# Result tiles inside the chunk's operand tile, result writes moved to the SyncE queue, and a reordered k.v schedule in a fused attention and expert kernel

## The chip, the cores and the metric

One Trainium2 chip, one core. The metric is device time of the program in microseconds (us): the median of the runs. Engines are named as in the profile: PE (TensorE matmul), PEld (its weight loads), DVE (VectorE), ACT (ScalarE), POOL (GpSimd), SP (SyncE). Every engine runs its instructions in program order; SP's instructions here are nearly all DMA issues.

## The reference

Linear attention over 8 batches, 8 heads, 576 tokens, head size 64, then two layers on the 4608 tokens of 512 features. Weights are 64-bit floats on entry.

```python
kv  = einsum('bhsd,bhse->bhde', k, v)
out = einsum('bhsd,bhde->bhse', q, kv)
x   = out / sqrt(mean(out*out, -1) + 1e-6) * g_norm      # per head
h   = ((x @ w1) * (x @ w2)) @ w3 ;  x = h @ w_out         # 512 -> 1024 -> 512
h   = x @ w_in ;  y = (h * sigmoid(h)) @ moe2_w_out       # 512 -> 2048 -> 512
```

## The kernel before, in words

**Stages.** A prologue multiplies w3 by w_out (tiles `wps`, to `wch`, `wcl`), unpacks the 64-bit weights (load, scale, tail, bits, high, low: `wide_*`) and computes attention of chunk 0. Tokens go in nine chunks of 512. Five chunks (`PLAIN` = 0, 1, 3, 5, 7) pass through the first layer at once; the other four (`LATER`) only get their attention here, which is written to DRAM (`xd`) and read back in the second half, which starts at about 468 us and which the change does not touch. All layer matmuls are done in three passes of high and low parts (`passes`, L150 to L152).

**The first layer's loop** has 5 x 8 steps. A step is: matmuls into `pa` (12), into `pb` (12), a first quarter of the previous step's product into `x2ps` (3), then the other three quarters (9). After the eighth step of a chunk the four `x2ps` banks (tag `acc`, 4 buffers) are copied out by ACT and DVE in turn, L702 and L704, to `x2o` tiles (3 buffers for 4 results) and written to `x2d` by DMAs of the POOL queue (L705).

**Events between the matmuls.** Each step has six slots; slot 6 x step + part is worked off after `pa` (parts 0 and 1), after `pb` (2), after the first quarter (3), and at the end of the step (4 and 5). `TIMES` gives for each kind of work the slots of its chunks or batches, the last entry of a row being that of chunk 8 (rows k and l count batches, and their last entry, for a batch 8, is not used): `a` (q times k.v on PE; ACT takes squares `sq` and copies `ob`, 4 buffers, in the order of `DRAIN` 0, 2, 3, 1), `c` (sums of squares on PE, tile `s`), `d`, `e` (the root on ACT and DVE), `r` (PE spreads the factors over `rb`; DVE multiplies into `ob`), `f0`, `f1` (chunk to the operand tiles `xh`, `xl`, or for LATER the DMA of `ob` to `xd`, L490, POOL queue), `k0`, `k3` (k.v matmuls of a batch's row tiles 0 to 2, and 3 and 4), `l0` to `l4` (loads of a batch's five row tiles of k and v, the last with 64 rows; 3 buffers each), `q0` to `q3` (loads of a chunk's q; 4 buffers). Within a slot the order is f0, f1, a, c, d, e, r, k, l, q. Tile buffers of one tag are taken in turn, so a load waits until the tile that had its buffer has been read.

**PSUM.** `pa` and `pb` share two banks (tag `ab`); `a` and `r` use two banks of `att` and these two as well; `s` and the k.v sum `kvps` each take an `att` bank.

**Weight pieces.** `advance()` works one piece of 64-bit weights on: write out what the last piece gave (`flush`, SP queue), load piece n+3 (`raw`, 3 buffers, 512 KB), scale piece n+1 on ACT, bits and differences on DVE. `PACE` says how many advances follow `pa`, the split, and again the split of each step. The first 14 pieces are w1 and w2 of the steps to come (two a step in the first chunk); later ones form blocks for the second half.

**The prologue** is an order by hand (`ORDER`).

Of the kernel before, what the change touches and what calls it, by code (L numbers as in the profile page):

```python
# [7 lines left out]
F32 = mybir.dt.float32  # L8
# [32 lines left out]
PACE = tuple(int(x) for x in """  # L41
# [5 lines left out]
""" if x.isdigit())  # L47
TIMES = {
# [18 lines left out]
}  # L67
# [27 lines left out]
ORDER = """  # L95
load0 load1 load2 kload0 scale0 tail0 load3 scale1 scale2 bits0 tailv1 highv0 tailv2 bits1 low0 kmm0
high1 kload1 low1 hh1 lh1 bits2 qload0 scale3 tail3 highv2 load4 kload2 low2 kmm1 bits3 scale4
hl1 tail4 qload3 highv3 kload3 lh2 kmm2 low3 qload2 qload1 kload4 bits4 high4 hh2 hl2 low4
hl3 kmm3 kmm4 kout0 load5 scale5 tailv5 lh3 bits5 load6 a0 b0 highv5 load7 low5 scale6
tailv6 bits6 scale7 hh3 load8 tail7 highv6 low6 bits7 a1 lh5 b1 high7 load9 scale8 hh5  # L100
c0 tailv8 hl5 hl7 low7 lh7 scale9 tailv9 load10 bits8 d0 bits9 kload5 hh7 load11 high8
scale10 tailv10 low8 load12 high9 e0 hh8 lh8 low9 eh0 bits10 load13 el0 scale11 tail11 high10
bits11 hl8 hl10 r0 low10 hh10 kload6 scale12 load14 tailv12 gload0 highv11 bits12 high12 low11 x0
lh10 lh11 load15 load16 scale13 low12 tail13 r1 hh11 bits13 x1 hl11 highv13 fh0 scale14 tail14
bits14 kload7 hl13 kmm5 scale15 fh1 kmm6 low13 tailv15 scale16 lh13 kload8 hh13 wh0 wh4 wh1
highv14 bits15 low14 kmm7 kload9 high15 wl0 wl1 low15 wh5 kmm8 kmm9 tail16 wl5 lh14 kout1
bits16 hl15 hl14 wl4 fl1 hh14 lh15 hh15 highv16 low16 fl0
"""


@with_exitstack
def fused(ctx, tc, q, k, v, g, w1, w2, w3t, wo1, wb, out):

# [5 lines left out]
    def pool(name, **how):  # L119
        opened[name] = tc.tile_pool(name=name, **how)  # L120
        return opened[name].__enter__()
# [39 lines left out]
    low = const.tile([P, 1], F32)  # L161
    const.tile([P, 79], F32, name="pad_left")
    spread = const.tile([P, P], F32R)
# [190 lines left out]
    def kv_load(b, js):  # L354
        for j in js:
            n = min(P, S - j * P)
            for nm, src in (("k", k), ("v", v)):
                t = at.tile([P, DM], F32, tag=nm, bufs=3, name=f"{nm}{b}_{j}")
                nc.sync.dma_start(out=t[:n], in_=src[b, j * P:j * P + n, :])
                kv_t[nm, b, j] = t, n  # L360

    kvps = {}

    def kv_mm(b, js):
        if js[0] == 0:
            kvps[b] = bank("att", 2, f"kvps{b}")
        for j in js:
            kt, n = kv_t.pop(("k", b, j))
            vt, _ = kv_t.pop(("v", b, j))

            for p in range(KD):
                for i in range(2):
                    f = slice((2 * p + i) * D, (2 * p + i + 1) * D)
                    nc.tensor.matmul(
                        out=kvps[b][i * D:(i + 1) * D, p * D:(p + 1) * D], lhsT=kt[:n, f], rhs=vt[:n, f],
                        start=(j == 0 and p == 0), stop=(j == 4 and p == KD - 1), skip_group_check=True)

    def kv_out(b):
        nc.scalar.copy(out=kv32[b % 2], in_=kvps.pop(b)[:, :KD * D].rearrange("p (a d) -> p a d", a=KD))
# [106 lines left out]
    def att_f(c, i, part=None, eng=None):  # L486
        ps_ = (2 * i, 2 * i + 1)
        if c in LATER:
            for p in ps_:
                nc.gpsimd.dma_start(out=xd[c][:, p, :], in_=o_t.pop((c, p)))  # L490
            return
        if i == 0 and part != 1:
            xt[c] = (xs.tile([P, KD, N], F32R, tag="xh", name=f"xh{c}"),
                     xs.tile([P, KD, N], F32R, tag="xl", name=f"xl{c}"))
        xh, xl = xt[c]
        for p in ps_:
            if part != 1:
                if eng is nc.vector:
                    eng.tensor_copy(out=xh[:, p, :], in_=o_t[c, p])
                else:  # L500
                    nc.scalar.copy(out=xh[:, p, :], in_=o_t[c, p])
            if part != 0:
                nc.vector.tensor_sub(out=xl[:, p, :], in0=o_t.pop((c, p)), in1=xh[:, p, :].bitcast(F32))
# [14 lines left out]

    more = [xs.tile([P, KD, N], U32, tag=x, name=f"more_{x}").rearrange("p a n -> p (a n)") for x in ("xh", "xl")]

# [116 lines left out]
    of["gload"] = g_load  # L637
    idle = at.tile([P, N], F32, tag="x2o", bufs=3, name="idle")
    nc.vector.memset(idle, 0.0)
# [11 lines left out]
    w12_tiles(w12b, range(2, K1))  # L651
    stg = pool(name="stg", bufs=3, reuse_waits="tile")
    cv = pool(name="cv", bufs=3, reuse_waits="tile")
# [32 lines left out]
    def g2_mm(c, j, ms):  # L686
# [6 lines left out]
        if j == K1 - 1 and ms[-1] == KD - 1:  # L693
            for m in range(KD):
                if c != PLAIN[-1]:
                    o = at.tile([P, N], F32, tag="x2o", bufs=3, name=f"x2o{c}_{m}")
                else:
                    if m == 0:
                        o4 = xs.tile([P, KD, N], F32, tag="xh", name=f"x2o{c}")
                    o = o4[:, m, :]  # L700
                if m % 2:
                    nc.vector.tensor_copy(out=o, in_=x2ps[c][m])  # L702
                else:
                    nc.scalar.copy(out=o, in_=x2ps[c][m])  # L704
                (nc.gpsimd if c != PLAIN[-1] else nc.scalar).dma_start(out=x2d[c][:, m, :], in_=o)  # L705
            del x2ps[c]

    def g1_mm(ps_out, wh, wl, xh, xl):
# [9 lines left out]
        "a": att_all, "c": att_c, "d": att_d, "e": att_norm, "r": att_spread,  # L718
        "k0": lambda c: kv_mm(c, [0, 1, 2]), "k3": lambda c: (kv_mm(c, [3, 4]), kv_out(c)),
    }  # L720
# [498 lines left out]
```

## Time and profile before

| | us |
|---|---|
| median of 3 runs (lowest, highest) | 1397.71 (1390.48, 1399.27) |
| profiled execution | 1394.57 |
| its span | 1392.8 |
| PE busy | 1369.9 |
| DVE, ACT, POOL busy | 870.8, 660.1, 347.4 |
| first `pa` matmul (end of the prologue) | 72.26 |

The sum of a prediction is made against the profiled execution, 1394.57 us, which is 1.8 us more than its span. A busy PE in this profile has its pipeline's overlap counted in, so one matmul is shown with 0.39 us although the next starts 0.23 us after it. The clock column (PEclk) is the share of the full TensorE clock that was granted.

### The profile page before, as it was taken

The page shows a single profiled execution, that of the slowest core. Times are in us where ns is not written, and L with a number is a line of the kernel's source. Part 1 is how long each engine was busy: PE and PEld are TensorE (multiplying, and loading weights), DVE is VectorE, ACT ScalarE, POOL GpSimd, SP SyncE. Part 2 cuts the span into 40 slices and gives each one's busy share as a digit, 9 for nine tenths or more (in the row PEclk, how much of TensorE's full clock was granted, in tenths as well). Part 3 has the DMA queues.
Part 4 walks back from the last instruction along what each step waited for, and adds up shares of the span by engine and source line. Part 5 has one row for each costly group of instructions (what it writes and reads, how often), then busy time and mean ns, then how long its engine had stood idle before and what let it go on. Part 6 is the DMA issues. An engine that isn't in the chain of part 4 may idle for free.

```text
span 1392.8 us, 19229 instructions
## 1 busy us (share of the span) xinstructions
PE 1369.9 (98%) x7012; PEld 1143.4 (82%) x7012; DVE 870.8 (63%) x1227; ACT 660.1 (47%) x1032; POOL 347.4 (25%) x238
## 2 busy tenths in 40 slices
PE   7999999999999999999999999999999999999998
PEld 4777777776777888887888888888888889999998
DVE  5955477475774547766764677455754576567468
ACT  5767455463662425514644354544534353543543
POOL 1000100001002040522522444224522352245222
PEclk9999999999999999999999999999999999999999
DMA  9854689897868497798688667866696668888886
GB/s 365 312 191 137 212 279 328 278 316 258 274 222 290 134 312 251 231 326 267 195 269 290 192 196 227 282 192 191 193 301 197 191 207 301 279 254 268 284 254 200
DMA packets 156109, 346.26 MB, mean 249 GB/s; under 512 B 15088, under 2 KB 73456, under 8 KB 156016
## 3 DMA queue, kind: packets, MB, share of 16 engines
q1 hardware_dynamic: 152880, 335.60, 74.5%
q0 software_dynamic: 2560, 8.39, 1.5%
q8 instruction: 56, 0.92, 0.3%
q10 hardware_dynamic: 576, 1.05, 0.2%
q14 instruction: 37, 0.30, 0.1%
HBM read 270.53 MB, written 74.45 MB: 248 GB/s over the span
## 4 chain that ended last, share of the span: by engine, by line
PE 83%; issue 12%; DMA 3%; DVE 1%; ACT 1%; POOL 0%; SPq 0%; DVEq 0%; POOLq 0%; ACTq 0%
PE ps L924 65%; PE wps L608 3%; PE x2ps L150 2%; PE pb L150 2%; PE pb L152 2%; PE pa L150 1%; PE pb L151 1%; PE pa L151 1%; PE pa L152 1%; PE x2ps L151 1%; PE x2ps L152 1%; DMA x2d<-x2o 1%; DMA v<-v_l 1%; DMA more_xl<-wo_l 1%; PE o L406 1%
## 5 line engine op out<-in xcount | busy, mean ns | idle before, releaser
L924 PE MATMUL ps<-xo,w 128*128 128x512 f32 (+1 forms) x2352 | 501.4, 373 | 1.1 <-ACT u L999 1.1
L924 PEld LDWEIGHTS ps<-xo,w 128*128 128x128 f32 x2352 | 431.9, 188 | 67.2 <-ACT u L999 1.5
L924 PE MATMUL ps<-go,w 128*128 128x512 f32 (+1 forms) x2016 | 425.4, 371 | 0.4 <-issue 0.4
L924 PEld LDWEIGHTS ps<-go,w 128*128 128x128 f32 x2016 | 368.7, 188 | 53.4 <-issue 1.0
L816 DVE TENSOR_TENSOR go<-g,go 128x1024 fp32r<-128x1024 f32 (+1 forms) x120 | 136.9, 1143 | 114.5 <-ACT go L815 113.5
L934 DVE TENSOR_TENSOR c<-ps,c 128x512 f32<-128x512 f32 (+1 forms) x280 | 171.2, 639 | 57.6 <-PE ps L924 56.9
L815 ACT CAST go<-g 128x1024 fp32r<-128x1024 f32 (+1 forms) x120 | 115.1, 980 | 49.5 <-PE ps L924 48.3
L803 POOL TENSOR_TENSOR g_t<-g 128x1024 f32<-128x1024 f32 (+1 forms) x48 | 111.1, 2315 | 75.3 <-DVE g L1006 70.4
L803 POOL TENSOR_TENSOR g<-g,g_t 128x1024 f32<-128x1024 f32 (+1 forms) x24 | 53.2, 2215 | 287.7 <-DVE go L816 287.7
L816 DVE TENSOR_TENSOR go<-g_t,go 128x1024 fp32r<-128x1024 f32 (+1 forms) x48 | 81.5, 1698 | 19.7 <-ACT go L815 19.7
L956 ACT COPY s<-ps 128x512 f32<-128x512 f32 (+1 forms) x40 | 21.7, 544 | 143.9 <-PE ps L924 143.9
L934 DVE TENSOR_TENSOR g<-ps,s 128x512 f32<-128x512 f32 (+1 forms) x48 | 30.2, 643 | 66.8 <-PE ps L924 60.7
L150 PE MATMUL x2ps<-ch,wch 128*128 128x512 f32 x160 | 65.4, 409 | 5.3 <-DVE x2o L702 5.3
L857 DVE TENSOR_TENSOR asb<-pb,asb 128x512 f32<-128x512 f32 x40 | 27.5, 688 | 65.9 <-PE pb L152 65.9
L150 PE MATMUL pa<-xh,w12h 128*128 128x512 f32 x160 | 65.0, 407 | 0.1
L151 PE MATMUL pa<-xl,w12h 128*128 128x512 f32 x160 | 63.9, 399 | 0.0
L152 PE MATMUL pa<-xh,w12l 128*128 128x512 f32 x160 | 63.8, 398 | 0.0
L146 DVE TENSOR_TENSOR cl<-asb,ch 128x512 fp32r<-128x512 f32 x40 | 28.2, 706 | 56.3 <-ACT ch L145 56.3
L150 PE MATMUL pb<-xh,w12h 128*128 128x512 f32 x160 | 63.0, 394 | 0.0
L152 PE MATMUL pb<-xh,w12l 128*128 128x512 f32 x160 | 62.5, 390 | 0.4 <-DVE w12l L268 0.4
L152 PE MATMUL x2ps<-ch,wcl 128*128 128x512 f32 x160 | 62.8, 392 | 0.0
L151 PE MATMUL x2ps<-cl,wch 128*128 128x512 f32 x160 | 62.7, 392 | 0.0
(141 smaller groups left out, 1734.1 us busy)
## 6 DMA issues: line engine op xcount, KB each, us to landing
w<-wbd SPq DMA_DIRECT2D x364, 512.0 KB, 4.3
wbd<-bh SPq DMA_DIRECT2D x60, 256.0 KB, 3.5
raw<-wb_l SPq DMA_DIRECT2D x24, 512.0 KB, 5.3
wbd<-s SPq DMA_DIRECT2D x48, 256.0 KB, 3.2
q<-q_l SPq DMA_DIRECT2D x36, 256.0 KB, 4.9
k<-k_l SPq DMA_DIRECT2D x32, 256.0 KB, 5.7
v<-v_l SPq DMA_DIRECT2D x32, 256.0 KB, 5.9
raw<-w_l SPq DMA_DIRECT2D x14, 512.0 KB, 4.8
```

What stands on the lines that cost most here:

```text
L146: nc.vector.tensor_sub(out=l, in0=x, in1=h.bitcast(F32))
L150: nc.tensor.matmul(out=ps_out, lhsT=ah, rhs=bh, start=first, stop=False)
L151: nc.tensor.matmul(out=ps_out, lhsT=ah, rhs=bl, start=False, stop=False)
L152: nc.tensor.matmul(out=ps_out, lhsT=al, rhs=bh, start=False, stop=last)
L608: nc.tensor.matmul(out=wps[m], lhsT=(l if which == "lh" else h)[:, x:x + P], rhs=rhs, start=left[m] == all_of, stop=left[m] == 1)
L803: nc.gpsimd.tensor_tensor(out=x, in0=x if a == place else self.src[a], in1=x if b == place else self.src[b], op=ALU.subtract)
L815: nc.scalar.copy(out=t[:, 0, :, :self.w], in_=x)
L816: self.cuts[n].tensor_tensor(out=t[:, 1, :, :self.w], in0=x, in1=t[:, 0, :, :self.w].bitcast(F32), op=ALU.subtract)
L857: nc.vector.tensor_mul(out=asb, in0=pb, in1=asb)
L924: mm = lambda a, bb, start, stop: nc.tensor.matmul(out=o, lhsT=a, rhs=bb, start=start, stop=stop, skip_group_check=True)
L934: eng.tensor_tensor(out=out_, in0=a, in1=b, op=ALU.add)
L956: nc.scalar.copy(out=t[nm, d], in_=o)
```

## The change

Four results of a chunk go into one tile `xo` that takes the place of the chunk's own `xh` (two tags `xh0`, `xh1` of one buffer each, in turn). They and the `xd` writes are issued by SP: `x2d` writes are put in the list that the next advance flushes, `xd` writes stand in `f0`, `f1`. k and v have 4 buffers; the 64-row tails of k and v lie side by side in DRAM and come in one DMA; two batches share the tile, on partitions 0 to 63 and 64 to 127. All five row tiles of a batch are multiplied in one run, in the slot of `c`. `raw` has 2 buffers. `TIMES`, `PACE` and `ORDER` are new.

```diff
 PACE = tuple(int(x) for x in """
-000 000 000 000 000 000 000 102
-000 121 100 111 002 231 000 113
-100 012 012 010 101 203 110 110
-112 100 030 110 211 000 221 100
-211 030 011 000 000 000 000 000
+000 000 000 000 000 000 000 101
+210 111 000 111 011 202 210 111
+101 003 004 001 100 312 001 000
+401 011 220 000 400 010 220 100
+202 031 011 000 000 000 000 000
...
 TIMES = {
-    "f0": (24, 43, 70, 106, 124, 186, 178, 213),
-    "f1": (25, 46, 72, 95, 127, 160, 182, 213),
-    "a": (2, 27, 57, 81, 111, 135, 165, 182),
-    "c": (9, 30, 65, 87, 116, 142, 171, 189),
-    "r": (15, 39, 69, 93, 123, 147, 177, 212),
-    "k0": (5, 43, 72, 98, 125, 151, 170),
-    "k3": (25, 52, 79, 107, 134, 158, 188),
-    "l0": (0, 16, 67, 84, 119, 142, 175),
-    "l1": (0, 23, 56, 86, 107, 134, 157),
-    "q2": (15, 35, 56, 97, 123, 151, 176),
-    "q3": (18, 29, 62, 90, 117, 158, 171),
+    "f0": (22, 47, 72, 103, 126, 154, 180, 206),
+    "f1": (25, 51, 74, 103, 135, 154, 182, 209),
+    "a": (8, 26, 57, 81, 111, 135, 164, 183),
+    "c": (17, 28, 67, 85, 117, 149, 166, 191),
+    "r": (21, 45, 69, 99, 123, 153, 177, 201),
+    "k": (17, 28, 67, 85, 117, 149, 166),
+    "l0": (5, 15, 29, 72, 109, 131, 163),
+    "l1": (0, 16, 56, 60, 86, 133, 161),
+    "q2": (19, 39, 62, 95, 111, 151, 175),
+    "q3": (18, 21, 50, 86, 108, 153, 166),
...
 ORDER = """
-load0 load1 load2 kload0 scale0 tail0 load3 scale1 scale2 bits0 tailv1 highv0 tailv2 bits1 low0 kmm0
-high1 kload1 low1 hh1 lh1 bits2 qload0 scale3 tail3 highv2 load4 kload2 low2 kmm1 bits3 scale4
-hl1 tail4 qload3 highv3 kload3 lh2 kmm2 low3 qload2 qload1 kload4 bits4 high4 hh2 hl2 low4
-hl3 kmm3 kmm4 kout0 load5 scale5 tailv5 lh3 bits5 load6 a0 b0 highv5 load7 low5 scale6
+load0 scale0 load1 load2 kload0 tail0 scale1 kmm0 kload1 load3 bits0 scale2 tail1 bits1 tail2 highv0
+high1 low1 kload2 lh1 hh1 bits2 load4 low0 scale3 tailv3 high2 hl1 low2 bits3 kmm1 kmm2
+kload3 scale4 tailv4 lh2 high3 bits4 low3 kmm3 hh2 hl2 kload4 high4 kmm4 qload0 load5 kout0
+qload1 scale5 low4 lh3 tailv5 load6 qload2 a0 bits5 qload3 hh3 b0 highv5 load7 scale6 low5
...
     def kv_load(b, js):
         for j in js:
-            n = min(P, S - j * P)
             for nm, src in (("k", k), ("v", v)):
-                t = at.tile([P, DM], F32, tag=nm, bufs=3, name=f"{nm}{b}_{j}")
-                nc.sync.dma_start(out=t[:n], in_=src[b, j * P:j * P + n, :])
-                kv_t[nm, b, j] = t, n
+                if j < 4:
+                    t = at.tile([P, DM], F32, tag=nm, bufs=4, name=f"{nm}{b}_{j}")
+                    nc.sync.dma_start(out=t, in_=src[b, j * P:(j + 1) * P, :])
+                    kv_t[nm, b, j] = t
+            if j == 4:
+                if b % 2 == 0:
+                    kv_t[b // 2] = at.tile([P, 2 * DM], F32, tag="kv4", name=f"kv{b}_{j}")
+                t = kv_t[b // 2][b % 2 * D:(b % 2 + 1) * D, :]
+                nc.sync.dma_start(out=t, in_=kv4[b])
+                kv_t["k", b, j], kv_t["v", b, j] = t[:, :DM], t[:, DM:]
...
         if c in LATER:
             for p in ps_:
-                nc.gpsimd.dma_start(out=xd[c][:, p, :], in_=o_t.pop((c, p)))
+                nc.sync.dma_start(out=xd[c][:, p, :], in_=o_t.pop((c, p)))
             return
         if i == 0 and part != 1:
-            xt[c] = (xs.tile([P, KD, N], F32R, tag="xh", name=f"xh{c}"),
+            xt[c] = (xs.tile([P, KD, N], F32R, tag=f"xh{PLAIN.index(c) % 2}", bufs=1, name=f"xh{c}"),
...
-    stg = pool(name="stg", bufs=3, reuse_waits="tile")
+    stg = pool(name="stg", bufs=2, reuse_waits="tile")
...
             for m in range(KD):
-                if c != PLAIN[-1]:
-                    o = at.tile([P, N], F32, tag="x2o", bufs=3, name=f"x2o{c}_{m}")
-                else:
-                    if m == 0:
-                        o4 = xs.tile([P, KD, N], F32, tag="xh", name=f"x2o{c}")
-                    o = o4[:, m, :]
+                if m == 0:
+                    xo = xs.tile([P, KD, N], F32, tag=f"xh{PLAIN.index(c) % 2}", bufs=1, name=f"xo{c}")
+                o = xo[:, m, :]
                 if m % 2:
                     nc.vector.tensor_copy(out=o, in_=x2ps[c][m])
                 else:
                     nc.scalar.copy(out=o, in_=x2ps[c][m])
-                (nc.gpsimd if c != PLAIN[-1] else nc.scalar).dma_start(out=x2d[c][:, m, :], in_=o)
+                if c == PLAIN[-1]:
+                    nc.scalar.dma_start(out=x2d[c][:, m, :], in_=o)
+                else:
+                    writes.append(dict(out=x2d[c][:, m, :], in_=o))
...
-        "k0": lambda c: kv_mm(c, [0, 1, 2]), "k3": lambda c: (kv_mm(c, [3, 4]), kv_out(c)),
+        "k": lambda c: (kv_mm(c, range(5)), kv_out(c)),
```

## Rows read from the trace of the kernel before

**Rows 1.** The page's first part: engine busy us (share of the span) xinstructions.
```profile
PE 1369.9 (98%) x7012; PEld 1143.4 (82%) x7012; DVE 870.8 (63%) x1227; ACT 660.1 (47%) x1032; POOL 347.4 (25%) x238
```

**Rows 2.** Windows: stretch, us, busy of each engine, PEclk, DMA share, GB/s.
```profile
9.20:72.20 63.00, 56.65 (x380) 41.84 (x381) 50.69 (x67) 41.31 (x60) 0.00 (x0) 1.00 0.95 353
```

**Rows 3.** Waits of PE: us in total, times, longest us.
```profile
PE kvps L374 <- DMA v<-v_l: 6.8, 5, 2.5
PE x2ps L150 <- DVE x2o L702: 5.3, 2, 3.3
PE wps L608 <- DVE woh L578: 1.9, 1, 1.9
```

**Rows 4.** Timeline of DVE and PE: start us, us, instruction [idle before <-releaser].
```profile
243.81 0.68 DVE L702 COPY x2o<-x2ps 128x512 f32<-128x512 f32 x1
...
249.07 0.69 DVE L702 COPY x2o<-x2ps 128x512 f32<-128x512 f32 x1 [4.58 <-DMA x2d<-x2o]
...
249.82 0.50 PE L150 MATMUL x2ps<-ch,wch 128*128 128x512 f32 x1 [2.00 <-DVE x2o L702]
...
336.75 0.79 PE L150 MATMUL x2ps<-ch,wch 128*128 128x512 f32 x1 [3.30 <-DVE x2o L702]
```

**Rows 5.** Windows behind the two waits for x2o, columns as in Rows 2.
```profile
250.60:257.30 6.70, 6.70 (x43) 5.34 (x43) 5.13 (x10) 2.35 (x5) 1.18 (x3) 0.50 0.85 278
...
336.80:342.60 5.80, 5.80 (x14) 4.54 (x15) 2.40 (x4) 0.62 (x1) 2.67 (x5) 0.50 1.03 361
```

**Rows 6.** Timeline of PE around three runs of k.v matmuls.
```profile
9.29 0.69 PE L374 MATMUL kvps<-v,k 128*64 128x64 f32 x16 [2.50 <-DMA v<-v_l]
9.91 0.96 PE L608 MATMUL wps<-woh,w3h 128*128 128x512 f32 x3
...
80.06 1.62 PE L374 MATMUL kvps<-v,k 128*64 128x64 f32 x48 [0.25 <-ACT ob L418]
81.60 0.50 PE L150 MATMUL pa<-xh,w12h 128*128 128x512 f32 x1
...
157.94 0.39 PE L151 MATMUL x2ps<-cl,wch 128*128 128x512 f32 x1
158.17 0.39 PE L152 MATMUL x2ps<-ch,wcl 128*128 128x512 f32 x1
158.49 1.30 PE L374 MATMUL kvps<-v,k 128*64 128x64 f32 x32
```

**Rows 7.** Timeline of PE, the last k.v tile of the prologue.
```profile
60.62 0.68 PE L374 MATMUL kvps<-v,k 64*64 64x64 f32 x16 [1.61 <-DMA v<-v_l]
```

**Rows 8.** Waits of the SP queue: us in total, times, longest us.
```profile
SPq L359 <- PE kvps L374: 44.1, 6, 16.0
...
SPq L198 <- ACT z L211: 24.7, 9, 4.5
...
SPq L383 <- PE o L406: 10.6, 2, 7.6
```

**Rows 9.** Timeline of PE, SP and ACT around `a` of chunk 3.
```profile
166.08 2.20 PE L406 MATMUL o<-q,kv 64*64 64x192 f32 x32
...
167.20 0.33 SPq L383 DMA_DIRECT2D q<-q_l  x1
...
168.66 0.61 ACT L418 COPY ob<-o 128x512 f32<-128x512 f32 x1
...
170.41 0.40 PE L150 MATMUL pa<-xh,w12h 128*128 128x512 f32 x1
```

**Rows 10.** DMA issues: out<-in queue xcount, KB each, median us to landing.
```profile
raw<-w_l SPq DMA_DIRECT2D x14, 512.0 KB, 4.8
...
x2d<-x2o ACTq DMA_DIRECT2D x4, 256.0 KB, 2.4
```

**Rows 11.** The tile `xd`: issue ns min/median/max, first and last; landing.
```profile
L490 POOL DMA_DIRECT2D xd<-ob x16: 539/539/689, 139.0 to 433.5; - x16
...
DMA to landing us min/median/max: 2.7/6.1/11.5
```

More of the change, by code (lines that the diff above doesn't have):

```diff
@@ L95, with fused @@
 ORDER = """
-load0 load1 load2 kload0 scale0 tail0 load3 scale1 scale2 bits0 tailv1 highv0 tailv2 bits1 low0 kmm0
-high1 kload1 low1 hh1 lh1 bits2 qload0 scale3 tail3 highv2 load4 kload2 low2 kmm1 bits3 scale4
-hl1 tail4 qload3 highv3 kload3 lh2 kmm2 low3 qload2 qload1 kload4 bits4 high4 hh2 hl2 low4
-hl3 kmm3 kmm4 kout0 load5 scale5 tailv5 lh3 bits5 load6 a0 b0 highv5 load7 low5 scale6
[L100 to L107, printed above, removed]
+load0 scale0 load1 load2 kload0 tail0 scale1 kmm0 kload1 load3 bits0 scale2 tail1 bits1 tail2 highv0
+high1 low1 kload2 lh1 hh1 bits2 load4 low0 scale3 tailv3 high2 hl1 low2 bits3 kmm1 kmm2
+kload3 scale4 tailv4 lh2 high3 bits4 low3 kmm3 hh2 hl2 kload4 high4 kmm4 qload0 load5 kout0
+qload1 scale5 low4 lh3 tailv5 load6 qload2 a0 bits5 qload3 hh3 b0 highv5 load7 scale6 low5
+tailv6 bits6 a1 scale7 highv6 load8 tailv7 load9 b1 bits7 hl3 lh5 c0 hh5 scale8 highv7
+low6 hl5 hl7 tail8 low7 scale9 tailv9 bits8 load10 bits9 d0 load11 high8 scale10 tailv10 e0
+low8 load12 high9 scale11 eh0 low9 tailv11 el0 load13 scale12 hh7 lh7 hh8 lh8 load14 bits10
+high10 r0 hl8 bits11 low10 highv11 tail12 bits12 hl10 load15 high12 kload5 lh10 scale13 low11 x0
+hh10 r1 tail13 lh11 load16 fh0 low12 hh11 bits13 x1 hl11 highv13 scale14 tail14 bits14 gload0
+scale15 hl13 kload6 tail15 kmm5 high14 fh1 low13 kmm6 lh13 kload7 hh13 wh1 low14 wh0 kload8
+bits15 kmm7 high15 wl0 wh4 scale16 wl1 kmm8 wh5 tailv16 low15 bits16 kload9 kmm9 lh14 hl14
+lh15 fl0 highv16 low16 hh15 hl15 wl5 hh14 wl4 fl1 kout1
 """
 @with_exitstack
-def fused(ctx, tc, q, k, v, g, w1, w2, w3t, wo1, wb, out):
+def fused(ctx, tc, q, k, v, kv4, g, w1, w2, w3t, wo1, wb, out):
     nc = tc.nc
@@ L161, in fused @@
     low = const.tile([P, 1], F32)
-    const.tile([P, 79], F32, name="pad_left")
+    const.tile([P, 72], F32, name="pad_left")
     spread = const.tile([P, P], F32R)
@@ L367, in kv_mm @@
         for j in js:
-            kt, n = kv_t.pop(("k", b, j))
-            vt, _ = kv_t.pop(("v", b, j))
+            kt, vt = (kv_t.pop((x, b, j)) for x in "kv")
             for p in range(KD):
@@ L374, in kv_mm @@
                     nc.tensor.matmul(
-                        out=kvps[b][i * D:(i + 1) * D, p * D:(p + 1) * D], lhsT=kt[:n, f], rhs=vt[:n, f],
+                        out=kvps[b][i * D:(i + 1) * D, p * D:(p + 1) * D], lhsT=kt[:, f], rhs=vt[:, f],
                         start=(j == 0 and p == 0), stop=(j == 4 and p == KD - 1), skip_group_check=True)
@@ L517, in of_pair @@
         return ts[j // 2][:, (j % 2) * N:(j % 2) * N + n * N]
-    more = [xs.tile([P, KD, N], U32, tag=x, name=f"more_{x}").rearrange("p a n -> p (a n)") for x in ("xh", "xl")]
+    more = [xs.tile([P, KD, N], U32, tag=x, bufs=n, name=f"more_{x}").rearrange("p a n -> p (a n)")
+            for x, n in (("xh1", 1), ("xl", 2))]
     def wide_load(n):
@@ L637, in fused @@
     of["gload"] = g_load
-    idle = at.tile([P, N], F32, tag="x2o", bufs=3, name="idle")
+    idle = at.tile([P, N], F32, tag="ob", bufs=4, name="idle")
     nc.vector.memset(idle, 0.0)
@@ L1194, in blocks, with rows @@
         return bits(np.concatenate([a, b]))
+    def rows(x):
+        return x.transpose(0, 2, 1, 3).reshape(B, S, DM)
     arrays = {
         "q_l": lay(q.transpose(1, 3, 0, 2).reshape(KD, P, NCH, N).transpose(2, 0, 1, 3)),
-        "k_l": lay(k.transpose(0, 2, 1, 3).reshape(B, S, DM)),
-        "v_l": lay(v.transpose(0, 2, 1, 3).reshape(B, S, DM)),
+        "k_l": lay(rows(k)[:, :4 * P]),
+        "v_l": lay(rows(v)[:, :4 * P]),
+        "kv4_l": lay(np.concatenate([rows(x)[:, 4 * P:] for x in (k, v)], axis=2)),
         "g_l": lay(g_norm),
```

14 rows, old and new, of the table TIMES are left out of this document.

## The prediction

> **What bounds the kernel now.** First the page's busy shares: PE works 1369.9 of 1392.8 us [rows 1]. So the kernel is bound by PE's own matmuls, and a change that removes no matmul can win only what PE loses: idle time (22.9 us), time at the lower clock, and time lost between matmuls. Then the waits of PE say whose fault the idle time is [rows 3]: 6.8 us for loads of v (prologue), 5.3 us for a DVE copy of a chunk's result, 1.9 us for an unpacked weight. The timeline of the 5.3 us shows two waits of 2.00 and 3.30 us, and what ended the first: the fourth copy to `x2o` sat 4.58 us idle, until the DMA that wrote the first result out had landed, because four results share three buffers [rows 4]. Last the granted clock: behind each of the two waits stands a stretch at 0.50 of 2.4 GHz, 1.2 GHz, of 6.7 and 5.8 us, in which PE has work all the time [rows 5]. At half clock half of it is lost, 3.4 and 2.9 us. After the waits of 1.9 and 1.61 us in the prologue [rows 3, 7] the window shows a clock of 1.00 [rows 2]. So a wait of two microseconds stands just where the trace shows the clock fall, and costs 3 us more if it does.
>
> **The change part by part.** The sum starts at this execution's 1394.6 us, 3.1 us under the median of 1397.71, which I read as spread (the three runs span 8.8).
>
> *Own tile for results.* All four copies can follow each other: the third ended at 243.81 + 0.68 = 244.49, a fourth of 0.69 ends at 245.18, and PE wanted that bank at 249.82 - 2.00 = 247.82 [rows 4], 2.6 us later. The tile's former content, `xh`, has been read by then, and the next writer of that tag is `f0` two PLAIN chunks on (results of chunk 0 at slots 48 to 53, `f0` of chunk 3 at 72), so no wait replaces the old one. Both waits go with their slow stretches: 2.00 + 3.30 + 3.4 + 2.9 = **-11.6 us**. What could be late next is DVE itself with more advances ahead of it; 2.6 us of cover are left, so I keep a low end of -6 (one of the two survives).
>
> *k.v in the run of the sums.* A run of these full-precision matmuls pays at both ends. Going in: 158.17 to 158.49 is 0.32 us against 0.23 between like matmuls, 0.09 more. Going out: a run of 16 takes 0.62 (9.29 to 9.91), one of 48 takes 1.54 (80.06 to 81.60), so 16 cost 0.46 and 0.16 belongs to the end [rows 6]. The loop has `k0` and `k3` for batches 2 to 7, twelve visits, one of which already stands against `a`; all now fall into the run of `c`: 11 x 0.25 = **-2.7 us** (-1.0 if only the entry is saved). The sums' chain to `r` is covered by the 80 matmuls of k.v.
>
> *Prologue.* The last k.v tile waited 1.61 us for v [rows 7], and the loads of k and v stood 44.1 us behind buffers not yet read, up to 16.0 at once [rows 8]. With four buffers a batch's loads find them free, so this 1.61 goes. Of the other prologue waits (6.8 - 1.61 of the v loads, 1.9 for the weight) 2.5 is the start, which keeps its order of loads. The remaining 2.7 of v and 1.9 compete for the same transfers at a DMA share of 0.95, and DVE is busy 50.69 of 63 us [rows 2]; moving loads forward moves others back. I take 0.9 of the 4.6: **-2.5 us** in all; ends -6.2 (all of it) and +2 (the new order makes PE wait for one more weight, as the 1.9 did).
>
> *Writes on SP.* 32 issues leave POOL, where each took 0.54 us [rows 11]; as SP issues of about 0.4 us they are 13 us of SP time over 310 us, in a queue that idles in waits. That by itself costs nothing. But a write now stands in line behind SP's waits, and at one place this counts. `q3` of chunk 4 is set at slot 50, but its buffer holds q of chunk 3, which is read by `a` at slot 57: SP stands there from 50 to 57. Such a wait exists before: 7.6 us [rows 8], ended by the same `a` (the load at 167.20 [rows 9]). Now `f1` of chunk 2, slot 51, is behind it: the writes of two `ob` tiles. And `a` of chunk 3 needs those very buffers for its second copy on ACT, and `pa` needs the bank which that copy frees. In the times of before: `a` ends at 166.08 + 2.20 = 168.28; q issue and write issue 0.8; landing; copy 0.61; `pa` would have started at 170.41 [rows 9]. For the landing the rows give 2.4 us (the same write on a quiet hardware queue [rows 10]) to 6.1 (median of these writes, which go out among others [rows 11]). SP has been standing, so I stay near the lower one and add 0.6 for the q load just ahead of it (256 KB at the 353 GB/s of the prologue is 0.7): 3.0. Then 168.28 + 0.8 + 3.0 + 0.61 = 172.7, about 0.4 of which the hand-overs overlap: **+1.9 us**, ends 1.3 and 5. The clock may fall or not; I forecast that it does not, and keep 3.4 us for the range.
>
> The Trainium skill (DMA: Bandwidth & Descriptors, section "Queues, rings and completion order") says that a DMA engine takes the descriptors of one ring in order and serves the rings in turn, so a write from POOL's ring would not sit behind SP's q load. By that rule these 0.6 us are the price of the move and the stall left on POOL's ring would be 1.3, the sum 1379.1; no row here separates the two.
>
> *Two raw buffers.* Load n+3 now waits for scale n+1 instead of n: one advance later. In the first chunk two advances fill a step of about 7.8 us, and the piece is scaled two advances after its issue: 7.8 us against a landing of 4.8 [rows 10]. Cover 3 us, cost nothing; beyond it ACT waits and weights come late: up to +2. SP already spends 24.7 us on this wait [rows 8]. Later pieces load in pairs with four advances between, where two buffers never meet.
>
> *One tail DMA a batch* is 8 issues less on SP, hidden like them; the 64-row matmuls stay. Nothing.
>
> Sum: 1394.6 - 11.6 - 2.7 - 2.5 + 1.9 = **1379.7 us**.
>
> **The rivals.**
> *Clock falls at the new wait* of `a`: 1379.7 + 3.4 = 1383.1. For it: it fell after 2.00 us. Against: it held after 1.9. Chance 0.25.
> *One more wait like it*: the new `PACE` has four advances in a row at slot 144 and a chunk end just behind, so either the old x2o wait survives once by DVE's queue, or an ACT wait for `raw` reaches PE. One wait of 2.0 with its 3.4: 1383.1 + 5.4 = 1388.5. Chance 0.17.
> *SP becomes the bound; slower.* All results, block writes and loads now pass one in-order queue, in which `l1` of batch 5 (slot 60) waits for the k.v of batch 4 (slot 67) and the like. If the raw load or a result write behind such a wait arrives after ACT's cover, PE stalls and the clock falls: 5.4 us each. With the prologue's loss of 2 instead of its gain (+4.5), and four such places: 1379.7 + 4.5 + 21.6 = 1405.8. It passes the profiled time from three places on. Against: in the trace SP stood 44.1 us for buffers [rows 8] and PE paid for it only in the prologue. Chance 0.07.
> *The change doesn't do what it says at `a`*: if the buffers free earlier than I read it, no wait, and the prologue wins all: 1394.6 - 11.6 - 2.7 - 6.2 = 1374.1. Chance 0.11.
>
> **How the numbers follow.** The forecast has 0.40, the rivals 0.25, 0.17, 0.07 and 0.11. A measurement of this kernel can tell about 1% from no change: 1383.7 is the line for faster, 1411.7 for slower. Faster: 0.40 (less 0.04 for its upper side), 0.11, and half of the 0.25 that sits on the line: 0.59. Slower: the upper part of the SP case, 0.04. Same: 0.37. The range from 1373 to 1392 leaves out the SP case and the tails of the outer two.
>
> **What would show it.** The idle time before L702 for its own write gone, and no stretch at 0.50 behind the ends of chunks 1 and 3; no separate k.v runs; first `pa` at about 69.8 instead of 72.3; a PE wait of about 1.9 us before `pa` of the step after `a` of chunk 3, ended by ACT's `ob`, itself ended by the DMA `xd`. If the `x2ps` wait remains, the step on the tile is wrong; if SP-issued writes land late in several places, the step on SP is.

## The result: 1374.3 us beside 1394.1, and the profile after

The changed kernel takes 1374.30 us (median of 4 runs, 1373.15 to 1376.72), the kernel before 1394.10 beside it: ratio 0.9859, 95% interval 0.9836 to 0.9881. The forecast was 1379.7, range 1373 to 1392. The profiled execution is the slowest of the four, 1376.72 with a span of 1374.9.

Busy time, first part of the page after, beside [rows 1]:

```profile
PE 1364.1 (99%) x7012; PEld 1142.5 (83%) x7012; DVE 873.9 (64%) x1225; ACT 661.2 (48%) x1034; POOL 331.5 (24%) x206
```

PE has the same 7012 matmuls and is idle for 10.8 us instead of 22.9. Its waits after, beside [rows 3]:

```profile
PE kvps L378 <- DMA v<-v_l: 3.7, 3, 2.2
PE idle_ps L647 <- DVE idle L644: 1.5, 1, 1.5
PE ps L929 <- ACT u L1004: 0.6, 1, 0.6
PE wps L613 <- DVE w3l L596: 0.5, 1, 0.5
```

No wait for `x2ps` is left. The windows (stretch, us, busy of PE, PEld, DVE, ACT, POOL, PEclk, DMA share, GB/s) show the first-layer loop (first `pa` to last `x2ps`) after and before, and the prologue after:

```profile
16.20:26.40 10.20, 9.46 (x52) 5.85 (x52) 4.62 (x7) 1.27 (x3) 0.00 (x0) 0.50 1.04 396
9.20:72.20 63.00, 59.60 (x365) 42.90 (x361) 49.09 (x65) 39.28 (x57) 0.00 (x0) 0.92 0.93 335
73.10:451.00 377.90, 377.58 (x2258) 295.66 (x2257) 235.96 (x433) 203.36 (x371) 10.77 (x4) 1.00 0.77 256
```
```profile
72.30:468.00 395.70, 388.05 (x2256) 298.96 (x2255) 232.71 (x431) 201.91 (x368) 26.95 (x36) 0.98 0.72 242
```

The loop went from 395.8 to 377.6 us: -18.2, all of the gain. PE now idles 0.3 us in it, at a clock of 1.00. The prologue of this execution lost 0.9 (first `pa` at 73.1, before 72.3), for with a wait of 2.24 us for v comes a stretch of 10.2 us at 0.50, which [rows 2] do not have. The rest is 0.5 shorter. Together -17.85 against the profiled 1394.57.

Where the 18.2 went is worked out from the starts of all PE matmuls of the loop, start to start, each compared with the usual step of its kind and place in a run: the two waits for `x2o` with their slow stretches [rows 4, 5] about -11.8, the edges of the k.v runs -3.4, `rb` -2.6, other short waits -0.4.

The chunk end that waited 2.00 us [rows 4] has its two DVE copies back to back now, and a batch's k.v stands in the run of the sums `s` (`kvps<-kv` is the tail tile of k and v). Timeline after of PE and DVE (start us, us, instruction), beside [rows 4, 6]:

```profile
121.09 1.06 PE L429 MATMUL s<-sq,ones 128*32 128x512 f32 x8
122.08 2.08 PE L378 MATMUL kvps<-v,k 128*64 128x64 f32 x64
124.10 0.68 PE L378 MATMUL kvps<-kv 64*64 64x64 f32 x16
124.71 0.50 PE L149 MATMUL pa<-xh,w12h 128*128 128x512 f32 x1
125.05 0.39 PE L150 MATMUL pa<-xl,w12h 128*128 128x512 f32 x1
125.28 0.39 PE L151 MATMUL pa<-xh,w12l 128*128 128x512 f32 x1
...
241.21 1.28 DVE L704 COPY xo<-x2ps 128x512 f32<-128x512 f32 x2
```

Around `a` of chunk 3, timeline after of SP, ACT and PE, beside [rows 9]:

```profile
165.72 0.35 SPq L387 DMA_DIRECT2D q<-q_l  x1
166.10 0.91 SPq L494 DMA_DIRECT2D xd<-ob  x2
...
166.22 0.58 ACT L422 COPY ob<-o 128x512 f32<-128x512 f32 x1
...
167.17 0.60 ACT L422 COPY ob<-o 128x512 f32<-128x512 f32 x1
...
168.69 0.40 PE L149 MATMUL pa<-xh,w12h 128*128 128x512 f32 x1
...
169.29 0.59 ACT L422 COPY ob<-o 128x512 f32<-128x512 f32 x1 [1.01 <-DMA xd<-ob]
```

SP stood 7.64 us until the q load (from the end of the issue before, at 158.07), as forecast; but the third copy waits for the write, not the second, and `pa` starts with no wait. SP's queue after, waits (us in total, times, longest), beside [rows 8]:

```profile
SPq L387 <- PE o L410: 16.9, 4, 7.1
SPq L358 <- PE kvps L378: 10.6, 2, 5.4
...
SPq L387 <- DMA v<-v_l: 3.3, 3, 1.4
...
SPq L358 <- DMA k<-k_l: 1.8, 3, 1.0
```

The standing for k.v fell from 44.1 to 10.6 us. e8b, with four k and v buffers under the old tables, has 0.3, so the buffers (or the single tail DMA beside them) took it, and the earlier load slots brought some back. The two rows that wait for another load are no buffer waits; the last section says what they are.

### The profile page after: what moved, and what is told of

Its sections match the earlier page's. It is cut to its first block, busy times and chain, and to the rows that moved or that the text cites. A ratio compares the mean times of both kernels' runs of the same rounds, so it can differ in the third digit from the quotient of the medians.

```text
span 1374.9 us, 19175 instructions
## 1 busy us (share of the span) xinstructions
PE 1364.1 (99%) x7012; PEld 1142.5 (83%) x7012; DVE 873.9 (64%) x1225; ACT 661.2 (48%) x1034; POOL 331.5 (24%) x206
## 4 chain that ended last, share of the span: by engine, by line
PE 96%; DMA 2%; DVE 0%; ACT 0%; SPq 0%; issue 0%; ACTq 0%; DVEq 0%
PE ps L929 66%; PE x2ps L149 3%; PE wps L613 3%; PE pb L151 3%; PE x2ps L150 3%; PE pa L149 3%; PE pb L149 3%; PE x2ps L151 3%; PE pb L150 3%; PE pa L150 3%; PE pa L151 3%; PE kvps L378 1%; PE o L410 1%; DMA wraw<-w3t_l 1%; PE s L429 1%; DMA kv<-kv_l 1%
## 5 line engine op out<-in xcount | busy, mean ns | idle before, releaser
L808 POOL TENSOR_TENSOR x_t<-x2r 128x1024 f32<-128x1024 f32 (+1 forms) x14 | 32.5, 2323 | 422.3 <-DMA w<-wbd 421.8
L144 ACT CAST ch<-asb 128x512 fp32r<-128x512 f32 x40 | 25.3, 633 | 78.4 <-DVE asb L862 78.4
```

Source lines behind the costliest of these rows:

```text
L144: nc.scalar.copy(out=h, in_=x)
L808: nc.gpsimd.tensor_tensor(out=x, in0=x if a == place else self.src[a], in1=x if b == place else self.src[b], op=ALU.subtract)
```

## The experiments

All times are medians; ratios are against the kernel before on the same chip, with 95% intervals. That kernel took 1394.0 us beside e1 to e4, 1391.4 beside e5 to e8b and 1393.6 beside e9 to e12, so differences between medians of different chips are good to 2 or 3 us only. "Loop" and "first `pa`" are from each one's profiled execution. The intervals of the kernels near 1374 overlap; differences of about 2 us between them are not resolved. Each loop is a single execution.

| | us | ratio | loop | first `pa` |
|---|---|---|---|---|
| before | 1394.1 | 1 | 395.8 | 72.3 |
| changed | 1374.30 | 0.9859 [0.9836, 0.9881] | 377.6 | 73.1 |
| e1 tile alone | 1388.89 | 0.9961 [0.9941, 0.9980] | 388.6 | 72.6 |
| e2 queue alone | 1392.18 | 0.9989 [0.9971, 1.0006] | 392.5 | 71.9 |
| e8b old tables | 1388.53 | 0.9973 [0.9954, 0.9993] | 385.7 | 74.7 |
| e11 three slots | 1386.09 | 0.9946 [0.9930, 0.9962] | 390.1 | 70.3 |
| e3 writes on POOL | 1376.31 | 0.9865 [0.9836, 0.9893] | 380.1 | 69.4 |
| e7 `f0` behind | 1377.30 | 0.9894 [0.9862, 0.9925] | 381.0 | 69.5 |
| e4 split runs | 1383.22 | 0.9917 [0.9885, 0.9948] | 383.7 | 70.3 |
| e12 `r` at 93 | 1373.72 | 0.9858 [0.9843, 0.9874] | 378.7 | 69.5 |
| e9 three raw | 1374.25 | 0.9863 [0.9843, 0.9882] | 377.5 | 71.2 |
| e5 old order | 1375.73 | 0.9875 [0.9844, 0.9906] | 376.8 | 70.5 |
| e6 late k.v | 1373.38 | 0.9863 [0.9833, 0.9894] | 377.6 | 70.0 |
| e10 k.v load first | 1375.39 | 0.9867 [0.9852, 0.9882] | 377.3 | 72.2 |

**e1, the tile alone**, on the kernel before (the tags of `xh` and of two prologue tiles change with it):

```diff
...
-                if c != PLAIN[-1]:
-                    o = at.tile([P, N], F32, tag="x2o", bufs=3, name=f"x2o{c}_{m}")
+                if m == 0:
+                    xo = xs.tile([P, KD, N], F32, tag=f"xh{PLAIN.index(c) % 2}", bufs=1, name=f"xo{c}")
+                o = xo[:, m, :]
...
```

> The kernel before with one part of the change: the four results of a chunk go into the chunk's own xh tile; their writes stay on POOL's queue, all tables are those of before. Theory (the tile removes the waits, the queue is not needed for that): both x2ps<-x2o waits (2.00 and 3.30 us) and the two stretches at 0.50 behind them are gone, 11.6 us less than before, about 1382 to 1384 beside 1394. Rival (the writes on POOL land so late that f0 of a later chunk waits for them, or the wait only moves): a wait of f0's ACT or DVE copy on DMA x2d shows, and less than 5 us is won. Second rival (the change of tables was needed as well): the gain is there, but another PE wait of 2 us or more takes part of it.

It wins 5 us (7.2 in the loop of the profiled execution), not 11.6: the second rival. The first wait and its stretch are gone; in the place of the second PE waits as long for something else. Timeline and window of e1:

```profile
337.78 1.30 PE L374 MATMUL kvps<-v,k 128*64 128x64 f32 x32 [3.28 <-DMA v<-v_l]
```
```profile
339.20:342.50 3.30, 3.30 (x9) 2.52 (x9) 2.42 (x6) 2.58 (x6) 0.00 (x0) 0.50 0.17 55
```

The loads of v for this run are issued at 325.8 and 328.5, and between 324.0 and 328.0 POOL issues the four results and three `xd` writes, now all at once. The tile `v` from 318 to 342 in e1:

```profile
DMA to landing us min/median/max: 9.1/9.2/9.4
```

Before, the fourth copy's wait held back both that burst and PE; the same v loads took 6.1 and 7.7 us, landed by 339.6, and were not needed until 345.9. The x2o wait had been hiding a late load.

**e2, the queue alone**: three x2o buffers, their writes on SP.

```diff
-                (nc.gpsimd if c != PLAIN[-1] else nc.scalar).dma_start(out=x2d[c][:, m, :], in_=o)
+                (nc.sync if c != PLAIN[-1] else nc.scalar).dma_start(out=x2d[c][:, m, :], in_=o)
```

> The kernel before with the queue alone changed: the writes of the results go out on SP's queue, still from three x2o buffers for four results; the xd writes stay on POOL. Theory (the buffers are the cause, the queue only shortens or lengthens the landing): the fourth copy still waits for the first write, PE waits 1 to 4 us at two or more chunk ends and the clock falls behind those over 2 us; the time is 1390 to 1400, within 5 us of before. Rival (POOL's late issue is the cause): the waits of 2.00 and 3.30 go, and the time is about 1383 as with the tile. Second rival: SP stands behind a buffer at a chunk end, and the wait grows beyond 4 us: slower than 1400.

The theory holds in the main: the time is not distinguishable from before, and DVE's fourth copy still waits for a write. But PE pays at one chunk end, where two or more were expected, with 5.05 us where at most 4 were expected; the wait of 2.00 [rows 4] is gone. Timeline of DVE and PE in e2:

```profile
333.31 0.69 DVE L702 COPY x2o<-x2ps 128x512 f32<-128x512 f32 x1 [8.50 <-DMA x2d<-x2o]
...
334.06 0.80 PE L150 MATMUL x2ps<-ch,wch 128*128 128x512 f32 x1 [5.05 <-DVE x2o L702]
```

**e8b, the changed tiles and buffers under the tables of before**: the changed kernel with `PACE`, `TIMES`, `ORDER` and the two runs `k0` and `k3` of the kernel before, and with the writes on POOL:

```diff
...
-nc.sync.dma_start(out=xd[c][:, p, :], in_=o_t.pop((c, p)))
+nc.gpsimd.dma_start(out=xd[c][:, p, :], in_=o_t.pop((c, p)))
-writes.append(dict(out=x2d[c][:, m, :], in_=o))
+nc.gpsimd.dma_start(out=x2d[c][:, m, :], in_=o)
...
```

> The changed kernel's tiles and buffers (results in the chunk's tile, four k and v buffers, one tail DMA, two raw buffers) with the tables of the kernel before (PACE, TIMES, ORDER, k.v in two runs), and with the writes on POOL's queue. Theory (the tables were needed too: the v load is issued too late by its slot, whatever the buffers): a PE wait for v of 1 to 3.5 us at the end of chunk 3 remains, and the time is 1385 to 1389, like the tile alone. Rival (four buffers suffice): no wait for v over 1 us in the loop, no stretch at 0.50, 1380 to 1384. Second rival (two raw buffers need the new PACE): ACT waits for raw and a new PE wait for asb or a weight of 1 us or more shows.

The theory holds: the wait for v shrinks and stays, without a slow stretch behind it. Timeline of e8b:

```profile
338.22 0.69 PE L379 MATMUL kvps<-v,k 128*64 128x64 f32 x16 [1.25 <-DMA v<-v_l]
```

So the buffers and the single tail DMA, which e8b does not tell apart, are part of the answer and the earlier load slots the rest: in the changed kernel the same batch's last loads land by 301.7 and are used at 313.6. Of the loop's 18.2, the tiles and buffers give 10.1 (to 385.7). The other 8.1 are the tables, with k.v in one run, and the move to SP together: 5.6 to e3 (380.1), whose writes are still on POOL, and 2.5 from there, which e3 does not resolve. The time gains only 2.9 us beside its own before (1391.4). Of the difference to the loop, 2.4 lie in the prologue of the profiled execution, where two stretches of 3.4 us at 0.50 stand behind waits of 1.57 and 1.94 us; the rest stays open.

**e11, three slots again under the new tables**, on e3:

```diff
-                o = xo[:, m, :]
+                o = xo[:, m if c == PLAIN[-1] else m % 3, :]
```

> The changed kernel with the writes on POOL's queue and the four results of a chunk put into three slots of the tile again: the fourth copy waits until the first write has been read out, as in the kernel before. Theory (the missing fourth buffer costs the waits, under the new tables as under the old): a PE wait before x2ps of 1.5 to 4 us, ended by that copy, at two to four chunk ends, with a stretch at 0.50 behind those over 2 us; 5 to 14 us more than with four slots and the writes on POOL (1376.3), so 1381 to 1390. Rival (the new PACE alone moved the chunk ends away from late landings): at most one wait under 1.5 us, and 1378 or less.

9.8 us more than e3, within the theory's 5 to 14, but paid elsewhere. DVE's waits (us in total, times, longest) and the timeline of DVE and PE in e11:

```profile
DVE xo L704 <- DMA x2d<-xo: 16.1, 4, 5.9
```
```profile
399.23 0.69 DVE L704 COPY xo<-x2ps 128x512 f32<-128x512 f32 x1 [4.00 <-DMA x2d<-xo]
...
401.93 0.75 DVE L457 SCALAR_TENSOR_TENSOR rhl<-u,low,rh 128x512 fp32r<-128x512 f32 x1 [0.69 <-ACT rh L453]
...
402.74 0.59 PE L467 MATMUL rb<-rhl,spread 32*128 32x512 f32 x3 [3.19 <-DVE rhl L457]
```

DVE stands at all four chunk ends (before: 4.57, 4.58, 6.74 and 0.79 us). Here PE wants `rb` before it wants the bank, and `rhl`, the operand of the `rb` matmuls, is made by DVE behind that copy: the same cause under another name, and a list of PE's waits alone would not have led to the tile. About 6.6 of the 10 us that the loop lost stand at this place (the wait and a stretch of 6.8 us at 0.50). About 3 more stand at 275, far from a chunk end, where `rb` waits 1.67 us for `asb` and a stretch of 3.4 us at 0.50 follows; e3 waits 0.57 us there, and why e11 waits longer stays open. (`asb` is the tile into which ACT copies `pa` and DVE multiplies `pb`; until then their banks are taken.)

**e3, the writes back on POOL**, on the changed kernel: the two write lines of e8b's diff.

> The changed kernel with the writes of x2d and xd given back to POOL's queue, all else as changed. Theory (in the sum the move to SP costs nothing for PE, and ACT's 1.0 us wait at `a` of chunk 3 comes from a write behind the blocked q load): that wait is gone or under 0.5 us, PE shows no new wait, and the time is that of the changed kernel within 2 us, about 1374. Rival (the move brought part of the 18 us that the loop won): 3 us or more of the loop come back, 1377 or more. Rival of the prediction's other side (SP's queue delays loads): 2 us or more less, 1372 or below.

ACT's wait at `a` is gone. The median is 2.0 us more (0.8 by the ratios), within the intervals; the loop is 2.5 longer, most of it by two new waits for `asb` (1.11 at 291.8 and 0.57 at 271.5) at places without a write. What the move to SP is worth by itself lies between nothing and about 2.5 us; these runs do not settle it.

**e7, `f0` of chunk 2 behind the q load**, on the changed kernel:

```diff
-    "f0": (22, 47, 72, 103, 126, 154, 180, 206),
+    "f0": (22, 51, 72, 103, 126, 154, 180, 206),
```

> The changed kernel with f0 of chunk 2 moved from slot 47 to 51, so that all four xd writes of the chunk stand behind the q load for which SP waits until `a` of chunk 3. Theory (the prediction's mechanism at `a` is right, and PE was spared only since two of the four buffers were written out ahead of that q load): the first ob copy of `a` of chunk 3 now waits for a landing about 3 us after the q load is released, PE waits 1.5 to 4 us before the next pa, with 0 to 4 us of lower clock behind it, and the time is 1376 to 1381. Rival (the copies of `a` have more slack than that): ACT waits, PE does not, and the time is that of the changed kernel within 1.5 us.

The mechanism of the prediction appears as soon as all four writes stand behind that load. Timeline of SP, ACT and PE in e7, and the window behind the wait:

```profile
162.03 0.34 SPq L387 DMA_DIRECT2D q<-q_l  x1
162.42 2.05 SPq L494 DMA_DIRECT2D xd<-ob  x4
...
165.75 0.59 ACT L422 COPY ob<-o 128x512 f32<-128x512 f32 x1 [3.11 <-DMA xd<-ob]
...
167.43 0.50 PE L149 MATMUL pa<-xh,w12h 128*128 128x512 f32 x1 [2.26 <-ACT ob L422]
```
```profile
168.90:172.20 3.30, 3.30 (x9) 2.58 (x8) 2.29 (x5) 2.76 (x6) 0.00 (x0) 0.50 1.00 342
```

2.26 us of wait and about 1.7 of slow clock (half of 3.4); the loop is 3.4 us longer, the median 3.0.

**e4, k.v split away from the sums**, on the changed kernel:

```diff
-    "k": (17, 28, 67, 85, 117, 149, 166),
+    "k0": (18, 30, 67, 86, 120, 150, 168),
+    "k3": (20, 32, 68, 88, 122, 152, 170),
```

> The changed kernel with a batch's k.v matmuls split again into two runs that stand away from the sums (three row tiles, then two), eleven runs more in the loop. Theory (a run of these matmuls costs 0.09 going in and 0.16 going out): 11 x 0.25 = 2.7 us more in the loop (3 with the slower first matmul behind a run), about 1377. Rival (the ends cost nothing, what the loop won came from the tables): the loop has the same length within 1 us. Second rival (the two visits hold the k and v buffers longer and SP stands longer): a load of raw or q comes late, and PE waits 1 us or more in a place of its own.

The loop is 6.1 us longer, twice the theory. Compared start to start, the edges of the eleven runs give 2.9 us of it, 0.27 each, about what the theory said. Idle time grows by 2.5, most of it in waits such as these, the first rows of a timeline of e4:

```profile
289.51 0.50 PE L150 MATMUL pb<-xh,w12h 128*128 128x512 f32 x1 [0.79 <-DVE asb L863]
...
295.96 0.86 PE L411 MATMUL o<-q,kv 64*64 64x384 f32 x8 [1.06 <-DVE asb L863]
```

The median is 8.9 us above the changed kernel, 2.8 more than the loop of the profiled execution explains (which is the fastest of its four); that part stays open.

**e12, `r` of chunk 4 back in slot 93**:

```diff
-    "r": (21, 45, 69, 99, 123, 153, 177, 201),
+    "r": (21, 45, 69, 93, 123, 153, 177, 201),
```

> The changed kernel with `r` of chunk 4 in slot 93, as before, instead of 99, one table entry. Theory (the waits of rb for asb in the kernel before came from the slots of r against DVE's backlog, and the new slots took them away): at that place the steps of rb grow by 0.4 to 1.5 us together with a wait for DVE's asb, nothing else moves, and the time stays within 1.5 us of the changed kernel, 1373 to 1377. Rival (the new PACE took them away, wherever r stands): rb's steps stay at 1.95 us for all 24.

A wait is back at that place, though for `rhl`, which DVE had not reached, and not for `asb`. Timeline of e12:

```profile
224.16 1.00 PE L467 MATMUL rb<-rhl,spread 32*128 32x512 f32 x4 [1.10 <-DVE rhl L457]
```

The slot counts, by DVE's backlog there; 1.1 us of loop, too little for the median. The other two `rb` waits of before were not tried in this way.

**e9, three raw buffers** (two more unused pads go as well, for room):

```diff
-    stg = pool(name="stg", bufs=2, reuse_waits="tile")
+    stg = pool(name="stg", bufs=3, reuse_waits="tile")
-    const.tile([P, 72], F32, name="pad_left")
...
```

> The changed kernel with three raw buffers again (some unused padding given up for their room). Theory (two buffers cost nothing: ACT's waits for raw are covered before PE): the loop has 377.6 us within 1 and the time is that of the changed kernel within 1.5, 1373 to 1376. Rival (ACT's waits for raw of 1.43 and 1.24 us are paid somewhere by PE): the loop is 1 to 2 us shorter. Second rival (earlier loads collide with those of k, v and q): a PE wait of 1 us or more for one of these shows.

The theory holds: ACT's waits for the later `raw` pieces are 8.0 us in all instead of 9.0, and neither loop nor time moves.

**e5, e6, e10, the prologue's order**: the `ORDER` of before; the last k.v matmuls later; the first k.v load earlier.

```diff
 e6:
-... kmm3 hh2 hl2 kload4 high4 kmm4 qload0 load5 kout0 qload1 scale5 low4 lh3 ...
+... hh2 hl2 kload4 high4 qload0 load5 qload1 scale5 low4 lh3 kmm3 kmm4 kout0 ...
 e10:
-load0 scale0 load1 load2 kload0 tail0 ...
+load0 scale0 kload0 load1 load2 tail0 ...
```

> The changed kernel with the prologue order of the kernel before (ORDER), all else as changed. Theory (the buffers, not the order, took the wait of 1.61 us for v; the order is worth about 1 us): the first pa stands at 70 to 72 us, the loop is as in the changed kernel (377.6 within 1), and the time is 1374 to 1377. Rival (the order alone wins, the buffers nothing): the wait of 1.6 us for v before the last k.v tile is back and the first pa stands at 72 or later. Second rival (the new order costs, its k.v matmuls stand too early for their loads): no wait for v over 1.5 us, no stretch at 0.50 in the prologue, first pa before 69.7, and the time 1373 or less.

> The changed kernel with the k.v matmuls of row tiles 3 and 4 and the copy of the sum moved behind lh3 in the prologue's order, just ahead of its `a`. Theory (the wait of 2.24 us for v before row tile 3 is due to the place of these matmuls alone, and the clock fell behind it): that wait is gone or under 0.7, no stretch at 0.50 in the prologue, first pa at 67.5 to 69.5, time 1370 to 1373. Rival (the transfers bound the prologue, whatever is multiplied first): another wait of the same size stands elsewhere, first pa at 69.7 to 73, time as the changed kernel within 1.5. Second rival (the matmuls were cover for the unpacking of the weights): waits for hh, hl or `a` grow, and it is 2 us or more slower.

> The changed kernel with the first loads of k and v moved ahead of the second and third weight load of the prologue. Theory (transfers bound the start: what comes earlier for k.v comes later for the weights): the first k.v run begins at 6.5 to 7.5 instead of 8.6, the first wps 1 us or more later, first pa at 69 to 71, and the time within 1.5 us of the changed kernel. Rival (PE's late start is the price, 1 to 3 us of waiting before the first k.v run, with the lower clock that stood behind it in the profile of the changed kernel): first pa at 67 to 68.5 and 1370 to 1372.5.

None differs from the changed kernel by more than the intervals allow. In e5 the wait of 1.61 us [rows 7] is gone under the old order, so the buffers or the single tail DMA took it, as the theory said. In e6 and e10 a wait leaves one place and comes back at another: timeline of e6, then waits of PE in e10.

```profile
21.66 1.19 PE L410 MATMUL o<-q,kv 64*64 64x512 f32 x8 [1.39 <-ACT kv L383]
...
25.47 1.08 PE L410 MATMUL o<-q,kv 64*64 64x512 f32 x4 [1.04 <-DMA q<-q_l]
```
```profile
PE wps L613 <- DVE w3l L596: 3.2, 1, 3.2
PE o L410 <- DMA q<-q_l: 2.2, 1, 2.2
```

With transfers busy for 0.92 or more of the stretch from 9.2 to 69.2 us in every one of these orders, an order chooses who waits. In e10 the first k.v matmul starts at 7.50 with no wait, and the first `wps` then waits 3.2 us. No version is distinguishably faster than the changed kernel.

## Why the prediction was right, and where it was not

The time is faster by over 1%, as I held likeliest, and within the range; 1374.3 is 5.4 us under the forecast, the time of the fourth rival (1374.1) but only half by its road: no wait at `a`, yes; a prologue that wins 6.2, no. That the total came out so near is partly luck: 2.6 us of `rb` stood in no term, the 1.9 of the stall did not come, and the prologue of the profiled execution took 3.4 us of this back.

**Own tile, -11.6: about -11.8 in the loop.** The waits and both stretches are gone, and e11 brings 9.8 us back through one index. What the step had wrong is what comes next: I named DVE; it was the load of v, which the second wait had covered (e1). The 11.6 is the gain of the tile with four k and v buffers and earlier load slots; the tile alone is worth 5. The prediction gave those edits no part in it.

**k.v in the run of the sums, -2.7: -3.4.** The mechanism was right, the term a little small. I took 0.09 going in and 0.16 going out. The rows after show a third piece: behind such a run the second matmul starts 0.34 us after the first (124.71 to 125.05), the next ones 0.23. Going out costs less than I took: 0.15 us pass from the last k.v matmul to the next one, and 0.03 of that is the usual step between k.v matmuls. 0.09 + 0.12 + 0.11 = 0.32 for a run that stands alone; eleven of them measure 0.31 each here and 0.27 in e4.

**Prologue, -2.5: +0.9 in the profiled execution, -1.1 to -2.8 in others.** The same order has its first `pa` between 69.4 and 71.2 in e3, e4, e7, e9, e11 and e12; I forecast 69.8. In the profiled execution the v load of row tile 3 landed late and the clock fell. The clock was the larger part: e3 waits 1.94 us at the same matmul, its clock stays at 1.00, and its first `pa` comes at 69.4. Timeline and window of e3:

```profile
17.24 0.69 PE L378 MATMUL kvps<-v,k 128*64 128x64 f32 x16 [1.94 <-DMA v<-v_l]
```
```profile
9.20:69.60 60.40, 57.19 (x381) 42.30 (x382) 49.99 (x67) 41.03 (x59) 0.00 (x0) 1.00 0.96 356
```

The late load did not wait for a buffer. Timeline of SP and PE in the changed kernel:

```profile
4.75 0.47 SPq L358 DMA_DIRECT2D k<-k_l  x1
6.16 0.33 SPq L358 DMA_DIRECT2D v<-v_l  x1
7.09 0.33 SPq L538 DMA_DIRECT2D more_xl<-wo_l  x1
7.85 0.33 SPq L358 DMA_DIRECT2D k<-k_l  x1
8.52 0.33 SPq L358 DMA_DIRECT2D v<-v_l  x1
...
16.94 1.12 PE L378 MATMUL kvps<-v,k 128*64 128x64 f32 x16 [2.24 <-DMA v<-v_l]
```

The landings of the second to fifth load are at 6.14, 7.07, 7.83 and 8.50: each of the last four issues starts 0.02 us after the landing of the load eight issues before it. The step "with four buffers a batch's loads find them free" overlooked that second limit. Whether an earlier issue would have won anything is not shown; in e10 it only moved the wait.

**Writes on SP, +1.9: 0.** SP's standing (7.64 us) and the landing (3.2, assumed 3.0) are as forecast, and ACT does wait for the write. The step that failed is that `a` "needs those very buffers for its second copy". `f0` had written out two buffers of the chunk before SP stood, the first and the last in the order of `DRAIN`, and the first two copies got those: here buffers went to the next tile in the order in which they were released, not strictly in turn as I had read it. The third copy paid 1.0 us on ACT. e7 removes that luck and shows the stall, 2.26 us. On rings, e7's first `xd` write landed 0.77 us after the q load ahead of it in SP's queue (164.96 and 165.73). The Trainium skill (DMA: Bandwidth & Descriptors, section "Queues, rings and completion order") has a DMA engine work through one ring in order, and this landing agrees. In e3 the POOL writes of the chunk landed by 152.4, long before the q load of 162.0, and ACT has no such wait: the stall that the prediction left on POOL's ring was not there, and no run here shows what another ring would have saved behind a q load.

**Two raw buffers, one tail DMA: 0.** So measured for the first (e9); the second was not taken apart. A step of the first chunk takes 9.75 us (78.0 us from 72.26 to 150.24, eight steps), not 7.8, so the cover was larger than I took.

**Not in the sum: `rb`, -2.6.** Its waits stood in the trace of before, short and scattered, as here in the waits of PE:

```profile
PE rb L463 <- DVE asb L857: 0.8, 2, 0.4
PE rb L463 <- DVE ob L470: 0.8, 1, 0.8
```

`rb` takes the banks of `ab`, which DVE must empty first. `r` kept its place within the step, and the prediction gave the new slots no term; but other slots meet another backlog (e12, which brings 1.1 of it back). Idle time is 1.6 of the 2.6; the rest is matmuls that start a little late.

**Two readings in the rivals.** "It held after 1.9" left out the stronger case in [rows 6]: a wait of 2.50 us, with the clock at 1.00 in the window of [rows 2]. And the rival of the slower SP queue passes the profiled time from two such places on (1395.0), not three.

## What to carry to other kernels

Before a wait is booked as a gain, look for what else arrives during it: a load that it covered can become the next wait (e1), and here only the edits that bring that load forward made the gain whole. A shared engine's queue moves a stall to whichever result PE wants next, so follow the stalled engine and not the name in PE's list of waits. Where several buffers of one kind come free one by one, ask how many of them are free at the stall, not whether the stall exists.

## What the runs showed of the hardware

SP's queue never had more than eight transfers under way: of the 923 issues of the changed kernel (899 before) none started before the landing of the one eight places ahead, and 37 (35) started within 0.06 us after it, while 146 (127) started before the landing of the seventh ahead. The eight is set by the program: in the traces' instruction records SP's issues use eight semaphores in turn (907 of 915 use that of the issue eight places ahead, before 883 of 891), and an issue waits for its semaphore while the transfer that had it is under way. The v load at 8.52 waits for the one that the load issued at 2.60 raises when it lands at 8.50. Whether the queue has a limit of its own is not told. Rows of SP that wait for another load, such as `SPq L387 <- DMA v<-v_l`, are of this kind.

The clock is not decided by the length of a wait alone. In the loops each of the seven waits of 1.67 to 5.05 us (before, e1, e2, e7, e11) goes with a stretch at 0.50 of 3.4 or 6.8 us. In the prologues both happen. At the first k.v matmul the clock stayed at 1.00 behind 2.50 us (before), 2.73 (e1) and 2.71 (e12), and fell behind 3.06 (e7), 2.88 (e9) and 2.06 (e11). It held behind 3.23 us ahead of the first `wps` in e10. Behind a wait of 1.94 us for `woh` it fell in e8b and held in the kernel before. I had priced a stretch at 3.4 us of loss from two cases; here it was at most 1.7 (3.4 us at half clock), 3.4 (6.8) or 5 (10.2), less where part of the stretch lies in the wait itself, as 2.9 of the 6.8 us in e2.
